# A convolution and spectral-mixing kernel: where the first transform's tiles run, a bank of transposes ahead of the last transform, and which engine clears two banks

## The chip, the cores and the metric

The kernel runs on one core of one Trainium2 chip. A time is the device time of one execution in microseconds (us). The core has five engines with queues of their own: TensorE (PE in the profile; its weight loads are PEld), VectorE (DVE), ScalarE (ACT), GpSimd (POOL) and SyncE (SP). [...] Matmul results land in PSUM, of which this kernel uses eight banks of 128 x 512 float32; VectorE and ScalarE read them out ("eviction").

## The reference

`x` is 8 x 3264 x 192 float32 (batch, row, channel). First a causal convolution with 7 taps runs along the rows; the 192 channels form 8 heads of 24, and the taps of a head are a softmax over 7 numbers. Then the first 64 frequencies of a real Fourier transform along the rows are mixed over channels with complex weights (64 matrices of 192 x 192, real and imaginary part), transformed back, added, and passed through a matrix with a rectifier:

```python
out = np.einsum('hk,bskhg->bshg', softmax(weight), x_unf)       # convolution, x = out
X = np.fft.rfft(x, axis=1)                                      # along the 3264 rows
Xr, Xi = np.real(X[:, :64]), np.imag(X[:, :64])
Yr = einsum('bmd,mde->bme', Xr, w_r) - einsum('bmd,mde->bme', Xi, w_i)
Yi = einsum('bmd,mde->bme', Xr, w_i) + einsum('bmd,mde->bme', Xi, w_r)
y = np.fft.irfft(Y, n=3264, axis=1)                             # Y is 0 above mode 63
u = x + y
result = u + np.maximum(u @ w_ch, 0.0)
```

## The kernel before

All work is bf16 in on-chip memory; the loads of `x` and of the weights are issued by GpSimd and change float32 into bf16 on the way. The order of the instructions on each engine is the order of the Python code (a manual schedule); semaphores only make an engine wait, they never reorder. The kernel has four stages.

*Convolution and forward transform.* The 8 batches are 4 pairs (`q` = 0 to 3), each cut into two units of row blocks; a block is 256 rows, and a pair has 26 tiles of 128 rows. Units 0 and 1 (pair 0) have 5 and 8 blocks, the others 7 and 6. GpSimd issues the loads of all units in order (`load_unit`, L152 and L156), then the weights. For each unit and head, `conv_step` makes eight short matmuls (L297) per half (`a` = 0, 1) against a band matrix, runs two steps behind itself for the upper rows (`CONVLAG = 2`), and evicts the result in place into `xall`: L334 on ScalarE or L336 on VectorE for pair 0, where one double-width PSUM tile holds both halves, L342 and L344 for the others, where each half has a bank of its own. Banks are taken from the front of the list `free` and put back at its end when evicted. For pair 0 the list holds four double banks, from unit 2 on eight single ones.

The forward transform of a pair is a sum over its 26 tiles of one matmul each (`dft`, L358) against the table `ftab` of sines and cosines. It is cut into two parts: the first goes to `xacc`, a stretch of `ct`, the second is added to it (L365). The table is made in six steps (`table`): steps 0 to 3 on VectorE (L197 to L204), the sine and cosine on ScalarE (L207, L209). `xtrans` (L377 to L388) turns the transformed rows and puts them into `xt`, the left operand of the mixing.

What stands around the change: 27 idle matmuls (L183) before the first convolution; after unit 0, ScalarE makes the first ten tiles' sines and cosines and TensorE runs 14 idle matmuls (L427). After unit 1, the PSUM pools are opened anew as eight single banks, in the order of their place and not of their release, and the ten tiles of unit 0 are transformed at once, into the first of these banks. The other 16 tiles of pair 0 follow after five heads of unit 2. For pairs 1 to 3 the parts are the tiles of their own two units; the last part of pair 3 (12 tiles) follows the last convolution.

*Transposes and mixing.* The pools are opened again: four banks for transposes (`zt4`), two (`ze`) and two (`zm`) for the mixing. Each mixing result fills only part of the partitions of `zm`, so two matmuls with a zero operand (L441) clear them. 16 groups of four modes (`mix`, L497, 24 matmuls for two groups) alternate with banks of transposes taken from a list (`tjobs`, L458): four banks of the table, one job that prepares `wsw`, and 39 banks of eight blocks of `xall`, written to `ct` (`c_bank`). A bank goes out by VectorE (L450) or, every third, by ScalarE (L448). Weights of groups 0 to 10 are loaded as early as there is room; group g + 11 is issued behind group g (L276). Each group's result passes through L507 or L509, a transpose, and L534 and L536 into `yet`.

*Way back.* Matmuls of `yet` with the channel matrix (L573, L574) begin after group 13 and run between groups 14 and 15.

*Output.* For each tile, L694 and L626 make the rectified and the plain part, L619 and L621 rectify, L606 adds, and SyncE stores.

Of the kernel before, what the change touches and what calls it, by code (L numbers as in the profile page):

```python
# [10 lines left out]
ACT = mybir.ActivationFunctionType  # L11
AX = mybir.AxisListType
F32 = mybir.dt.float32
BF16 = mybir.dt.bfloat16
# [6 lines left out]
def kernel(  # L21
# [9 lines left out]
    nc = tc.nc  # L31
    B, S, D = x.shape
    H, KK = weight.shape
# [4 lines left out]
    P = 128  # L38
    NQ = B // 2
    NB = S // (2 * P) + 1  # L40
    NT = 2 * NB
# [3 lines left out]
    BW = P + 2  # L45
    TWOPI = 6.283185
    MAGIC = 12582912.0
    NIDLE = 27
    UNITS0 = ((0, 5), (5, 8))
    UNITS = ((0, 7), (7, 6))  # L50
    units = [(q, b0, n) for q in range(NQ) for b0, n in (UNITS if q else UNITS0)]
# [11 lines left out]
    xall = sb("xall", [NSLOT, 2, D], BF16)  # L63
    ct = sb("ct", [NQ * NT * 3, P], BF16)
# [76 lines left out]

    ctx.enter_context(tc.manual_schedule())

    free = open_psum("left", (2, 2)) + open_psum("right", (2, 2))

    def load_unit(q, b0, n):
        nf = min(n, NB - 1 - b0)
# [44 lines left out]
    def table(step, t0, t1):  # L192

        n = t1 - t0
        tu, wh = tu3[:, t0:t1, :], wh3[:, t0:t1, :]
        if step == 0:
            nc.vector.tensor_tensor(out=tu, in0=sidx[:, t0:t1].unsqueeze(2).to_broadcast([P, n, MODES]),  # L197
                                    in1=midx.unsqueeze(1).to_broadcast([P, n, MODES]), op=ALU.mult)
        elif step == 1:
            nc.vector.tensor_scalar(out=wh, in0=tu, scalar1=MAGIC, scalar2=-MAGIC, op0=ALU.add, op1=ALU.add)  # L200
        elif step == 2:
            nc.vector.tensor_tensor(out=tu, in0=tu, in1=wh, op=ALU.subtract)
        elif step == 3:
            nc.vector.tensor_scalar(out=wh.bitcast(U32), in0=tu.bitcast(U32), scalar1=0x7FFFFFFF, scalar2=None,  # L204
                                    op0=ALU.bitwise_and)
        elif step == 4:
            nc.scalar.activation(out=ftab[:, t0:t1, 1:2 * MODES:2], in_=tu, func=ACT.Sin, scale=-TWOPI)  # L207
# [96 lines left out]
    def conv_step(u):  # L304

        lower = upper = iter(())
        flow.append(None)
        if u is not None:
            if u[0]:
                z = free.pop(0)  # L310
            else:
                z = flow[-2][0][2] if u[4] else free.pop(0)
            flow[-1] = [(u, z[:, u[4] if u[0] == 0 else 0, :], z), []]
            lower = conv_pieces(flow[-1][0], 0)
        old = flow[-1 - CONVLAG] if len(flow) > CONVLAG else None
# [12 lines left out]
        s0 = NT * q + 2 * b0  # L328
        dst = xall[:, s0:s0 + 2 * n, :, GRP * h:GRP * h + GRP].rearrange("p (b a) i e -> p a b i e", a=2)
        tile0 = flow[-2 - CONVLAG][0][2]  # L330
        if q == 0:
            srcv = tile0[:, :, 0:2 * GRP * n].rearrange("p a (b i e) -> p a b i e", b=n, i=2)
            if b0 == 0 or h % 2:
                nc.scalar.copy(out=dst, in_=srcv)  # L334
            else:
                nc.vector.tensor_copy(out=dst, in_=srcv)  # L336
            free.append(tile0)
        else:
            for a, z in enumerate((tile0, tile1)):
                srcv = z[:, 0, 0:2 * GRP * n].rearrange("p (b i e) -> p b i e", b=n, i=2)  # L340
                if a == 1:
                    nc.scalar.copy(out=dst[:, a], in_=srcv)  # L342
                else:
                    nc.vector.tensor_copy(out=dst[:, a], in_=srcv)  # L344
                free.append(z)

    def flush():
        for _ in range(CONVLAG):
            conv_step(None)
        flow.clear()  # L350

    def dft(q, t0, t1):

        z = free.pop(0)
        xp = z[:, 0, 0:2 * D]
        for t in range(t0, t1):
            k = PL if t >= NT - 2 else P
            nc.tensor.matmul(xp, ftab[0:k, t, :], xall[0:k, NT * q + t, :, :],  # L358
                             start=(t == t0), stop=(t == t1 - 1), skip_group_check=True)
        if t0 == 0 and q == 0:  # L360
            nc.vector.tensor_copy(out=xacc, in_=xp)
        elif t0 == 0:
            nc.scalar.copy(out=xacc, in_=xp)
        else:
            nc.vector.tensor_tensor(out=xs[q % 2][:, :, :].rearrange("p i d -> p (i d)"), in0=xp, in1=xacc, op=ALU.add)  # L365
        free.append(z)

    def xtrans(q, banks=None):
# [12 lines left out]
        for i in range(2):  # L381
# [5 lines left out]
            else:  # L387
                nc.scalar.copy(out=dst, in_=srcv)  # L388

    todo = []  # L390
    pend = []

    def dfts():
        while todo:
            q, t0, t1 = todo.pop(0)
            dft(q, t0, t1)
            if t1 == NT:
                pend.append(q)

    P1, P2 = (0, 2 * UNITS0[0][1]), (2 * UNITS0[0][1], NT)  # L400
    nc.vector.tensor_scalar(out=sidx, in0=sidx, scalar1=1.0 / S, scalar2=None, op0=ALU.mult)
    for part in (P1, P2):
        for step in range(4):
            table(step, *part)

    for k, u in enumerate(units):
        for h in range(H):
            for a in range(2):
                conv_step((*u, h, a))
            if k > 1 and h == (4 if k == 2 else 2):  # L410
                if pend:
                    xtrans(pend.pop(0))
                dfts()
        if k == 2:
            for g in range(NW + NL):
                load_w(g)
        todo.append((u[0], 2 * u[1], 2 * (u[1] + u[2])))
        if u[0]:
            continue

        flush()
        for step in (4, 5):
            table(step, *(P1, P2)[k])
        if k == 0:
            z = free.pop(0)
            for _ in range(14):
                nc.tensor.matmul(z[:, 0, :], band[:, 0, 0, 0:P], band[:, 0, 0:1, 0:P].to_broadcast([P, 4, P]), start=True,  # L427
                                 stop=True, skip_group_check=True)
# [4 lines left out]
    flush()  # L433
    dfts()
    nc.gpsimd.memset(yet[:, :, 2 * B * (MODES - 8):2 * B * MODES], 0.0)
    zt4 = open_psum("left", (1, 1, 1, 1))
# [1 line left out]
    ze, zm = [z[:, 0, :] for z in z4[0:2]], [z[:, 0, :] for z in z4[2:4]]  # L438
    for z in zm:

        nc.tensor.matmul(z[:, 0:2 * D], w1[0:64, 0:P], w1[0:64, :], start=True, stop=True, skip_group_check=True)  # L441
    tbank = [0]
    ncopy = [1]

    def copy(out, in_):
        ncopy[0] += 1
        if ncopy[0] % 3 == 0:
            nc.scalar.copy(out=out, in_=in_)  # L448
        else:
            nc.vector.tensor_copy(out=out, in_=in_)  # L450

    def next_bank():
        k = tbank[0] % 4
        tbank[0] += 1
        return zt4[k][:, 0, :].bitcast(BF16)

    def trans(o, in_):
        nc.tensor.matmul(o, in_, ident[:], start=True, stop=True, is_transpose=True)  # L458
# [7 lines left out]
    def c_bank(k0):  # L466
        tp = next_bank()
        for k in range(8):
            qt, w = divmod(k0 + k, 3)
            row = xall[:, qt, :, :].rearrange("p i d -> p (i d)")  # L470
            trans(tp[:, P * k:P * k + P], row[:, P * w:P * w + P])
        copy(ct[:, k0:k0 + 8, :].rearrange("p t s -> p (t s)"), tp[:, 0:8 * P])

    def w_bank():

# [307 lines left out]
```

## Time and profile before

| what | value |
|---|---|
| time, median of 3 runs (lowest to highest) | 174.47 us (174.03 to 174.59) |
| the profiled execution | 174.49 us, span 172.7 us |
| busy share of the span | PE 95%, DVE 74%, ACT 65%, POOL 32% |
| granted TensorE clock, mean | 0.996 |
| first convolution (L297) starts | 10.42 us |
| unit 1's convolution starts | 18.01 us |
| first mixing group (L497) starts | 74.81 us |
| HBM read, written | 39.10 MB, 20.05 MB |

The span runs from the first to the last instruction of the execution that was profiled; all positions in the text are microseconds from its start. A group line of the profile reads: line, engine, operation, output <- inputs, shapes, count, then busy time, mean duration in ns, and the idle time of that engine just before, with what ended it. A line of a timeline reads: start, duration, engine, line, operation, count, and in brackets the idle time before it and its releaser. Durations of matmuls overlap, so a group's extent over its count is the pace, not the mean. A line of the chain of waits is start, duration and what the path that ended last was doing there.

### The profile page before, as it was taken

The page shows a single profiled execution, that of the slowest core. Times are in us where ns is not written, and L with a number is a line of the kernel's source. Part 1 is how long each engine was busy: PE and PEld are TensorE (multiplying, and loading weights), DVE is VectorE, ACT ScalarE, POOL GpSimd, SP SyncE. Part 2 cuts the span into 40 slices and gives each one's busy share as a digit, 9 for nine tenths or more (in the row PEclk, how much of TensorE's full clock was granted, in tenths as well). Part 3 has the DMA queues.
Part 4 walks back from the last instruction along what each step waited for, and adds up shares of the span by engine and source line. Part 5 has one row for each costly group of instructions (what it writes and reads, how often), then busy time and mean ns, then how long its engine had stood idle before and what let it go on. Part 6 is the DMA issues. An engine that isn't in the chain of part 4 may idle for free.

```text
span 172.7 us, 6812 instructions
## 1 busy us (share of the span) xinstructions
PE 163.5 (95%) x2847; PEld 131.3 (76%) x2847; DVE 128.3 (74%) x258; ACT 112.6 (65%) x222; POOL 54.4 (32%) x93
## 2 busy tenths in 40 slices
PE   6999979999999999899999989999999999999980
PEld 2375757768778687589999965699899989999950
DVE  4899755457566584377777756799999999999990
ACT  8469177247366375177776744678888888878860
POOL 7999923324323354244441000890000000000000
PEclk9999999999999999999999999999999999999998
DMA  2999999999999999999999930489989899899995
GB/s 31 201 204 203 204 203 203 204 205 199 205 203 204 208 207 209 203 207 206 206 207 207 206 58 0 156 289 342 339 314 360 313 349 353 321 351 332 352 344 188
DMA packets 37359, 40.14 MB, mean 232 GB/s; under 512 B 2480, under 2 KB 37328, under 8 KB 37328
## 3 DMA queue, kind: packets, MB, share of 16 engines
q0 software_dynamic: 22816, 19.62, 70.9%
q1 hardware_dynamic: 14512, 20.09, 31.8%
q8 instruction: 22, 0.36, 0.8%
q14 instruction: 9, 0.07, 0.1%
HBM read 39.10 MB, written 20.05 MB: 342 GB/s over the span
## 4 chain that ended last, share of the span: by engine, by line
PE 82%; DMA 7%; DVE 3%; POOL 2%; ACT 2%; issue 1%; DVEq 0%; POOLq 0%; ACTq 0%
PE z L694 34%; PE z L297 18%; PE z L458 11%; PE z L358 10%; DMA xall<-in_x_dram 7%; PE z L497 3%; POOL xall L152 2%; DVE xall L344 1%; PE z L626 1%; PE z L573 1%; PE z L574 1%; PE z L377 1%; DVE arena L606 1%; PE z L564 1%; ACT ftab L448 1%
## 5 line engine op out<-in xcount | busy, mean ns | idle before, releaser
L606 DVE TENSOR_TENSOR arena<-z,xall 128x384 f32<-128x384 f32 (+1 forms) x104 | 57.0, 557 | 3.8 <-PE z L694 1.9
L619 ACT ACTIVATE z<-z 128x384 f32<-128x384 f32 x102 | 48.2, 475 | 12.8 <-PE z L694 3.7
L694 PE MATMUL z<-arena,ftab 64*128 64x384 bf16 x308 | 45.3, 322 | 0.0
L694 PEld LDWEIGHTS <-ct 64*128 64x128 bf16 x600 | 42.3, 94 | 3.3 <-PE z L626 0.6
L297 PE MATMUL z<-xall,shared 64*64 64x336 bf16 (+3 forms) x1024 | 37.9, 294 | 0.2 <-DMA xall<-in_x_dram 0.2
L694 PE MATMUL z<-wsw,ct 64*128 64x192 bf16 x300 | 37.4, 243 | 0.0
L297 PEld LDWEIGHTS <-shared 64*64 64x64 bf16 x1024 | 32.7, 106 | 5.7 <-issue 2.9
L694 PE MATMUL z<-wm,ct 64*128 64x192 bf16 x200 | 31.4, 243 | 0.0
L344 DVE CAST xall<-z 128x336 bf16<-128x336 f32 (+1 forms) x48 | 22.9, 483 | 11.1 <-PE z L297 8.8
L694 PEld LDWEIGHTS <-ftab 64*128 64x128 bf16 x396 | 28.7, 93 | 2.8 <-issue 1.0
L342 ACT CAST xall<-z 128x336 bf16<-128x336 f32 (+1 forms) x48 | 20.1, 419 | 13.2 <-PE z L297 8.4
L694 PE MATMUL z<-w,ct 64*128 64x192 bf16 x100 | 24.3, 243 | 0.0
L450 DVE COPY ct<-z 128x1024 bf16<-128x1024 bf16 x26 | 17.8, 689 | 5.7 <-PE z L458 4.2
L458 PE MATMUL z<-ident,xall 128*128 128x128 bf16 x312 | 19.9, 219 | 0.0
L358 PE MATMUL z<-xall,ftab 128*128 128x384 bf16 (+1 forms) x104 | 18.3, 326 | 1.4 <-ACT xall L334 0.9
L458 PEld LDWEIGHTS <-xall 128*128 128x128 bf16 x312 | 17.8, 98 | 0.9
L152 POOL DMA_DIRECT2D xall<-in_x_dram x16 | 14.9, 939 | 6.9 <-DMA xall<-in_x_dram 6.0
L448 ACT COPY ct<-z 128x1024 bf16<-128x1024 bf16 x13 | 13.2, 1013 | 4.9 <-PE z L458 4.9
L358 PEld LDWEIGHTS <-ftab 128*128 128x128 bf16 (+1 forms) x104 | 9.7, 98 | 8.7 <-issue 2.7
L694 PE MATMUL z<-mixa,ftab 64*128 64x384 bf16 x88 | 13.8, 323 | 0.1
L521 POOL DMA_DIRECT2D arena<-xs x16 | 7.9, 504 | 17.1 <-ACT xs L517 17.1
L334 ACT CAST xall<-z 128x480 bf16<-128x480 f32 (+1 forms) x12 | 7.0, 660 | 5.9 <-PE z L297 5.9
(112 smaller groups left out, 153.9 us busy)
## 6 DMA issues: line engine op xcount, KB each, us to landing
out_dram<-arena SPq DMA_DIRECT2D x47, 384.0 KB, 3.5
xall<-in_x_dram POOLq DMA_DIRECT2D x8, 672.0 KB, 16.1
xall<-in_x_dram POOLq DMA_DIRECT2D x8, 480.0 KB, 16.7
arena<-in_moe_w_r_dram POOLq DMA_DIRECT2D x10, 288.0 KB, 11.3
arena<-in_moe_w_i_dram POOLq DMA_DIRECT2D x10, 288.0 KB, 11.3
ct<-in_moe_w_r_dram POOLq DMA_DIRECT2D x6, 288.0 KB, 11.7
ct<-in_moe_w_i_dram POOLq DMA_DIRECT2D x6, 288.0 KB, 11.9
out_dram<-arena SPq DMA_DIRECT2D x3, 288.0 KB, 2.9
```

What stands on the lines that cost most here:

```text
L152: nc.gpsimd.dma_start(out=xin[:, s0:s0 + nf, 2 * D * i:2 * D * (i + 1)], in_=src)
L297: yield nc.tensor.matmul(o, band[r, h, int(a != a1), c0:c0 + 64], xin5[r, s1:s1 + n, :, a1, dsl], start=(row == 0 and a1 == 0), stop=(row ...
L342: nc.scalar.copy(out=dst[:, a], in_=srcv)
L344: nc.vector.tensor_copy(out=dst[:, a], in_=srcv)
L358: nc.tensor.matmul(xp, ftab[0:k, t, :], xall[0:k, NT * q + t, :, :], start=(t == t0), stop=(t == t1 - 1), skip_group_check=True)
L448: nc.scalar.copy(out=out, in_=in_)
L450: nc.vector.tensor_copy(out=out, in_=in_)
L458: nc.tensor.matmul(o, in_, ident[:], start=True, stop=True, is_transpose=True)
L521: nc.gpsimd.dma_start(out=zwl[k:k + 1, :, :, :].rearrange("p b t d -> p b (t d)"), in_=ylate[r + 2:r + B, :])
L606: nc.vector.tensor_tensor(out=o[0:pn, :, a, :], in0=bank[0:pn, 0:2 * D].rearrange("p (i d) -> p i d", i=2), in1=xall[0:pn, s + a, :, :], o ...
L619: nc.scalar.activation(out=z, in_=z, func=ACT.Relu)
L694: mm = nc.tensor.matmul(target(bank[k], cols, r), l, r, start=first, stop=last, skip_group_check=True)
```

## The change

Five edits, named by the lines before:

- The forward transform of pair 0 is cut at tile 6 instead of tile 10. Its first part (`PA`, six tiles) runs directly after unit 0, between four and three idle matmuls in place of 14; `xacc` is then written by ScalarE. The other 20 tiles run at the place in unit 2 where 16 ran. Nothing is transformed between units 1 and 2.
- The table is made in three parts (6, 10 and 10 tiles) whose steps are spread: VectorE makes `PA` before the first eviction, the others between and behind the evictions of unit 0; ScalarE makes the sine of `PA` after its fifth eviction.
- In unit 0 heads 5 and 7 are evicted by VectorE instead of ScalarE; in unit 1 the even heads go to ScalarE and the odd ones to VectorE, the other way round than before. The opening has 24 idle matmuls instead of 27.
- After unit 1 the eight single banks are listed in the order in which their double banks came free.
- One `c_bank` (blocks 8 to 15) runs between the last convolution and the last transform, in a bank of the list `free`, and leaves the list `tjobs`. The two clearing matmuls become two ScalarE activations of scale 0. `copy` counts this bank, so that in the mixing stage the copies change engine one bank later than before.

```diff
-    NIDLE = 27
+    NIDLE = 24
-    free = open_psum("left", (2, 2)) + open_psum("right", (2, 2))
+    twos = open_psum("left", (2, 2)) + open_psum("right", (2, 2))
+    free = list(twos)
...
-            if b0 == 0 or h % 2:
+            if h not in (5, 7) if b0 == 0 else h % 2 == 0:
                 nc.scalar.copy(out=dst, in_=srcv)
...
-        if t0 == 0 and q == 0:
-            nc.vector.tensor_copy(out=xacc, in_=xp)
-        elif t0 == 0:
+        if t0 == 0:
             nc.scalar.copy(out=xacc, in_=xp)
...
+    def c_bank(k0, tp=None):
+        tp = next_bank() if tp is None else tp
...
-    P1, P2 = (0, 2 * UNITS0[0][1]), (2 * UNITS0[0][1], NT)
+    PA, PB, PC = (0, 6), (6, 16), (16, NT)
     nc.vector.tensor_scalar(out=sidx, in0=sidx, scalar1=1.0 / S, scalar2=None, op0=ALU.mult)
-    for part in (P1, P2):
-        for step in range(4):
-            table(step, *part)
+    for step in range(4):
+        table(step, *PA)
+    chores = {(0, 0): [(PB, (0,))], (0, 5): [(PA, (4,))], (0, H): [(PA, (5,)), (PB, (1, 2, 3)), (PC, range(4))],
+              (1, H): [(PC, (4, 5))]}
+    def tables(*place):
+        for part, steps in chores.get(place, ()):
+            for step in steps:
+                table(step, *part)
...
             for a in range(2):
                 conv_step((*u, h, a))
+            tables(k, h)
...
         flush()
-        for step in (4, 5):
-            table(step, *(P1, P2)[k])
+        tables(k, H)
         if k == 0:
-            z = free.pop(0)
-            for _ in range(14):
-                nc.tensor.matmul(z[:, 0, :], band[:, 0, 0, 0:P], ...
-            free.append(z)
+            idle(4)
+            dft(0, *PA)
+            for step in (4, 5):
+                table(step, *PB)
+            idle(3)
         else:
-            free[:] = open_psum("left", (1, 1, 1, 1)) + open_psum("right", (1, 1, 1, 1))
-            dft(*todo.pop(0))
+            ones = open_psum("left", (1, 1, 1, 1)) + open_psum("right", (1, 1, 1, 1))
+            free[:] = [ones[2 * twos.index(z) + i] for z in free for i in range(2)]
+            todo.append((0, PA[1], NT))
     flush()
+    z = free.pop(0)
+    c_bank(8, z[:, 0, :].bitcast(BF16))
+    free.append(z)
     dfts()
...
     for z in zm:
-        nc.tensor.matmul(z[:, 0:2 * D], w1[0:64, 0:P], w1[0:64, :], start=True, stop=True, skip_group_check=True)
+        nc.scalar.activation(out=z[:, 0:2 * D], in_=ident[:, 0:1].to_broadcast([P, 2 * D]), func=ACT.Copy, scale=0.0)
...
-    tjobs += [(c_bank, k) for k in range(0, 3 * NT * NQ, 8)]
+    tjobs += [(c_bank, k) for k in range(0, 3 * NT * NQ, 8) if k != 8]
```

`idle(n)` is the loop of idle matmuls as a function of their number.

More of the change, by code (lines that the diff above doesn't have):

```diff
@@ L388, in xtrans, with copy, trans @@
                 nc.scalar.copy(out=dst, in_=srcv)
+    ncopy = [1]
+    def copy(out, in_):
+        ncopy[0] += 1
+        if ncopy[0] % 3 == 0:
+            nc.scalar.copy(out=out, in_=in_)
+        else:
+            nc.vector.tensor_copy(out=out, in_=in_)
+    def trans(o, in_):
+        nc.tensor.matmul(o, in_, ident[:], start=True, stop=True, is_transpose=True)
+    def c_bank(k0, tp=None):
+        tp = next_bank() if tp is None else tp
+        for k in range(8):
+            qt, w = divmod(k0 + k, 3)
+            row = xall[:, qt, :, :].rearrange("p i d -> p (i d)")
+            trans(tp[:, P * k:P * k + P], row[:, P * w:P * w + P])
+        copy(ct[:, k0:k0 + 8, :].rearrange("p t s -> p (t s)"), tp[:, 0:8 * P])
     todo = []
@@ L398, in dfts, with idle @@
                 pend.append(q)
-    P1, P2 = (0, 2 * UNITS0[0][1]), (2 * UNITS0[0][1], NT)
+    PA, PB, PC = (0, 6), (6, 16), (16, NT)
     nc.vector.tensor_scalar(out=sidx, in0=sidx, scalar1=1.0 / S, scalar2=None, op0=ALU.mult)
-    for part in (P1, P2):
-        for step in range(4):
-            table(step, *part)
+    for step in range(4):
[6 more added lines that the diff above has]
+                table(step, *part)
+    def idle(n):
+        z = free.pop(0)
+        for _ in range(n):
+            nc.tensor.matmul(z[:, 0, :], band[:, 0, 0, 0:P], band[:, 0, 0:1, 0:P].to_broadcast([P, 4, P]), start=True,
+                             stop=True, skip_group_check=True)
+        free.append(z)
     for k, u in enumerate(units):
@@ L416 @@
                 load_w(g)
-        todo.append((u[0], 2 * u[1], 2 * (u[1] + u[2])))
         if u[0]:
+            todo.append((u[0], 2 * u[1], 2 * (u[1] + u[2])))
             continue
         flush()
-        for step in (4, 5):
-            table(step, *(P1, P2)[k])
+        tables(k, H)
         if k == 0:
-            z = free.pop(0)
-            for _ in range(14):
-                nc.tensor.matmul(z[:, 0, :], band[:, 0, 0, 0:P], band[:, 0, 0:1, 0:P].to_broadcast([P, 4, P]), start=True,
-                                 stop=True, skip_group_check=True)
-            free.append(z)
-        else:
-            free[:] = open_psum("left", (1, 1, 1, 1)) + open_psum("right", (1, 1, 1, 1))
-            dft(*todo.pop(0))
+            idle(4)
[3 more added lines that the diff above has]
+            idle(3)
+        else:
+            ones = open_psum("left", (1, 1, 1, 1)) + open_psum("right", (1, 1, 1, 1))
+            free[:] = [ones[2 * twos.index(z) + i] for z in free for i in range(2)]
+            todo.append((0, PA[1], NT))
     flush()
+    z = free.pop(0)
+    c_bank(8, z[:, 0, :].bitcast(BF16))
+    free.append(z)
     dfts()
@@ L439 @@
     for z in zm:
-        nc.tensor.matmul(z[:, 0:2 * D], w1[0:64, 0:P], w1[0:64, :], start=True, stop=True, skip_group_check=True)
+        nc.scalar.activation(out=z[:, 0:2 * D], in_=ident[:, 0:1].to_broadcast([P, 2 * D]), func=ACT.Copy, scale=0.0)
     tbank = [0]
[L443 to L450, printed above, removed]
     def next_bank():
@@ L455, in next_bank @@
         return zt4[k][:, 0, :].bitcast(BF16)
-    def trans(o, in_):
-        nc.tensor.matmul(o, in_, ident[:], start=True, stop=True, is_transpose=True)
     def g_bank(t0, n):
@@ L464, in g_bank @@
         copy(ftab[:, t0:t0 + n, :].rearrange("p t s -> p (t s)"), tp[:, 0:P * n])
[L466 to L472, printed above, removed]
     def w_bank():
```

## The prediction

> **What bounds the kernel now.** I read the page first (busy time, slices, chain by line), then the chain of waits piece by piece, then the timelines of single engines around each edit, last the issues and landings of the weight loads.
>
> ```profile
> PE 163.5 (95%) x2847; PEld 131.3 (76%) x2847; DVE 128.3 (74%) x258; ACT 112.6 (65%) x222; POOL 54.4 (32%) x93
> ...
> GB/s 31 201 204 203 204 203 203 204 205 199 205 203 204 208 207 209 203 207 206 206 207 207 206 58 0 156 289 342 339 314 360 313 349 353 321 351 332 352 344 188
> ...
> PE z L694 34%; PE z L297 18%; PE z L458 11%; PE z L358 10%; DMA xall<-in_x_dram 7%; PE z L497 3%; POOL xall L152 2%; DVE xall L344 1%; PE z L626 1%; PE z L573 1%; PE z L574 1%; PE z L377 1%; DVE arena L606 1%; PE z L564 1%; ACT ftab L448 1%
> ```
>
> TensorE is busy 95% and its lines carry the chain; work taken off it before the output stage looks worth its full length. But the GB/s row is flat at about 205 from slice 2 to slice 23 (some 99 us): the loads of x and then of the weights run without a hole, whatever TensorE does. So the question is how close the weights' landings lie to the matmuls that use them (L497). Its last groups in TensorE's timeline, with what ScalarE does between them:
>
> ```profile
> 96.58 0.70 PE L497 MATMUL z<-arena,mixa 128*16 128x192 bf16 x24
> ...
> 98.32 1.01 ACT L448 COPY ct<-z 128x1024 bf16<-128x1024 bf16 x1 [0.48 <-PE z L458]
> ...
> 99.23 0.27 ACT L536 COPY yet<-z 128x128 bf16<-128x128 bf16 x1
> ...
> 100.28 0.47 PE L497 MATMUL z<-arena,mixa 128*16 128x192 bf16 x12
> ...
> 103.61 0.46 PE L497 MATMUL z<-arena,mixa 128*16 128x192 bf16 x12
> ```
>
> The first row is groups 12 and 13 of the 16 weight groups (12 matmuls each), so group 13 starts 0.35 in, at 96.93; the others are groups 14 and 15. The second half of group 13 was issued at 84.98, that of group 15 at 91.05 (GpSimd's timeline), and the issue view gives their times to landing:
>
> ```profile
> 84.98 0.61 POOL L276 DMA_DIRECT2D arena<-in_moe_w_i_dram  x1 [0.56 <-DMA ct<-in_moe_w_i_dram]
> ```
> ```profile
> 91.05 0.61 POOL L276 DMA_DIRECT2D arena<-in_moe_w_i_dram  x1 [0.55 <-DMA arena<-in_moe_w_i_dram]
> ```
> ```profile
> arena<-in_moe_w_i_dram POOLq DMA_DIRECT2D x1, 288.0 KB, 11.5
> ```
> ```profile
> arena<-in_moe_w_i_dram POOLq DMA_DIRECT2D x1, 288.0 KB, 11.1
> ```
>
> Group 13 is complete at 84.98 + 11.5 = 96.5, group 15 at 91.05 + 11.1 = 102.2, group 14 about halfway, at 99.3. The slack before the matmuls is 0.4, 1.0 and 1.4 us. That is the core of this prediction: TensorE can come early by 0.4 us at group 13 and not more.
>
> **The change, part by part.** GpSimd's and SyncE's queues keep their instructions, their order and their waits; each weight issue waits for the landing eight loads earlier (the releasers above), so nothing here makes the loads end sooner.
>
> *Six tiles in the wait for rows.*
>
> ```profile
> 24.16 0.81 ACT xall L334
> ...
> 25.02 1.78 PE z L358 x10
> 26.80 2.97 PE z L297 x72
> ```
> ```profile
> 14.58 3.19 PE L427 MATMUL z<-shared 128*128 128x512 bf16 x14
> 18.01 6.12 PE L297 MATMUL z<-xall,shared 64*64 64x384 bf16 x128 [0.23 <-DMA xall<-in_x_dram]
> ```
> ```profile
> 11.60 3.80 ACT L334 CAST xall<-z 128x480 bf16<-128x480 f32 x8 [1.38 <-PE z L297]
> 15.43 0.92 ACT L207 ACTIVATE ftab<-arena 128x640 bf16<-128x640 f32 x1
> ```
>
> Between 14.58 and 18.01 TensorE runs 14 idle matmuls (0.23 each) until rows land. After: 4 idle ones (to 15.5), six tiles (1.78/10 = 0.178 each, 1.1), 3 idle ones. The tiles need cosines: five evictions (0.475 each, to 14.0), a sine for six tiles (between 0.92 x 384/640 = 0.55 and 0.92; 0.63 taken), the seventh eviction, a cosine: ready at about 15.75, tiles done at 16.9, idle ones at 17.6. The rows' landing hides all this; only 0.4 us of slack is left, and what runs over 18.0 delays the second unit one for one. Three of the opening 27 idle matmuls go; the first convolution waits for ScalarE's bands, so at most 0.1, swallowed by the same landing.
>
> *The second unit and what follows.*
>
> ```profile
> L152 POOL DMA_DIRECT2D xall<-in_x_dram x2: 957/974/992, 6.3 to 7.2; - x2
> ...
> DMA to landing us min/median/max: 14.6/15.8/17.0
> ```
>
> Now the convolution ends at 24.13, the eviction at 24.16 holds its bank until 25.0, ten tiles run, and unit 2 starts at 26.8. After the change nothing stands between: banks are taken in the order in which they came free, and unit 2 starts when its rows are in, at 7.2 + 17.0 = 24.2, say 24.35. Gain 2.4. Four of these ten tiles move into the second pair's transform (20 tiles for 16): 4 x 0.178 = 0.7 back. ScalarE now makes the last ten tiles' sines and cosines (two of about 0.95) as unit 2 starts, and its first eviction there comes late by up to 1 us; eight banks absorb between all and half of that: 0 to 0.5. Front gain 1.2 to 1.7; I take 1.5. Evictions that alternate engines the other way, and the DVE table steps spread behind them, I cost at nothing: the convolution between 18.0 and 24.1 covers them, with a ring of four double banks; were the ring full, each microsecond of a late eviction would be one on the path.
>
> *The last transform.*
>
> ```profile
> 69.79 2.11 PE L358 MATMUL z<-xall,ftab 128*128 128x384 bf16 x12 [0.55 <-DVE xall L344]
> 71.83 0.49 PE L441 MATMUL z<-w 64*128 64x384 bf16 x2
> ```
> ```profile
> 72.01 0.56 DVE L365 TENSOR_TENSOR xs<-z,ct 128x384 bf16<-128x384 f32 x1 [2.27 <-PE z L358]
> ```
> ```profile
> 73.36 1.01 ACT L448 COPY ftab<-z 128x1024 bf16<-128x1024 bf16 x1 [3.69 <-PE z L458]
> 74.27 0.48 ACT L388 CAST mixa<-z 128x384 bf16<-128x384 f32 x1
> ```
> ```profile
> 106.85 0.47 ACT L619 ACTIVATE z<-z 128x384 f32<-128x384 f32 x1 [0.85 <-PE z L626]
> ```
>
> ```profile
> L450 DVE COPY ct<-z 128x1024 bf16<-128x1024 bf16 x26 | 17.8, 689 | 5.7 <-PE z L458 4.2
> L458 PE MATMUL z<-ident,xall 128*128 128x128 bf16 x312 | 19.9, 219 | 0.0
> ```
>
> Eight transposes now fill the 0.55 us in which TensorE waits for the last evictions (eight take 8 x 19.9/312 = 0.5): no cost, and one bank less later. The two clearing matmuls (0.43 on the path) go to ScalarE, but one cleared bank is the one the last transform used, so the clears wait for DVE's sum, 72.01 + 0.56 = 72.57. Two clears of that shape (0.47 each by the nearest row, 0.4 at least) end at 73.4, when the table copy starts today (73.36); then comes the 0.48 copy that releases the first L497. So this edit gains 0 (from -0.2 to +0.1).
>
> *The mixing stage.* TensorE enters it 1.5 us early, runs as tightly as before (copies alternate in another phase, same load), reaches group 13 at 95.4 and waits for its landing: start 96.5, not 96.93, which is 0.4 kept and 1.1 lost. From there to group 14 one bank of transposes fewer remains. Today ScalarE's 1.01 copy at 98.32 delays its L536 copy to 99.23, which the next matmuls wait for. After, ScalarE copies the first of two banks and DVE the second, in 0.69. Counted from the end of group 13, DVE's part is ready at 1.0 + 0.7 + 0.2 = 1.9 against ScalarE's 2.2 today (99.50 - 97.28), so about 0.25 more is gained. Group 14 then starts at about 99.65, after its landing (99.3); group 15 follows 3.3 later at 102.95, after 102.2. The rest is the same work.
>
> **Sum:** 0.4 + 0.2 = 0.6 us off the profiled 174.49 (span 172.7 and 1.8 around it; the median of the runs is 174.47): 173.9. With landings 0.3 earlier or later, 173.5 to 174.2. About 0.3%, 0.52 us, is what a measurement of this kernel can tell from no change, so this sits at that edge.
>
> [...]
>
> **Rivals.**
> *A, no floor:* the loads move with TensorE or the landings I read are not what L497 waits for. Then 1.5 plus one bank (0.5) stays: 174.49 - 2.0 = 172.5. Against it: eight loads in flight and a flat rate. Chance 0.17.
> *B, a later floor:*
>
> ```profile
> q8 instruction: 22, 0.36, 0.8%
> ```
>
> Code fetches take 0.8% of 16 x 172.7 us over 22 packets, 1.0 us of one engine each. One more ahead of a last piece puts a landing up to 1 us later; before, slack hid that, now nothing does: up to 174.8, no measurable change. Chance 0.18.
> *C, slower: a slow clock.* The opening idle matmuls show two rates (the first six, then the last seven):
>
> ```profile
> L183 PE MATMUL z<-xall 128*128 128x512 bf16 x6 | 2.7, 630 | 1.6 <-DVE xall L170 1.6
> ```
> ```profile
> L183 PE MATMUL z<-xall 128*128 128x512 bf16 x7 | 1.7, 379 | 0.0
> ```
>
> 0.45 against 0.24 us each. Fewer idle matmuls, and three waits of up to 0.7 us (one for the three taken off the opening, two about the six tiles), could drop TensorE to the slow rate. Unit 1 (6.1 us) would then take up to 5.2 more: 174.49 - 1.5 + 5.2 - 0.25 = 177.9. It decides for slower once over 2.3 us are lost, about 2.7 us at the slow rate. Against: after the opening no gap of the trace shows it. Chance 0.13 (with other losses of that size).
> [...]
>
> **How the numbers follow.** The forecast has 0.52, of which 0.35 lies below 173.95 (0.3% faster) and 0.17 within. Faster: 0.35 + A 0.17 = 0.52. Same: 0.17 + B 0.18 = 0.35. Slower: C, 0.13. The range runs from A's 172.5, taken at 172.6, to B's 174.9.
>
> **What would show it.** Right: unit 2's convolution starts at 24.3 to 24.5; the first L497 at about 73.3; TensorE waits about 1 us for a weight load between groups 12 and 13, at 96.5; the weight issues and landings stay within 0.3 us. Wrong: group 13 runs at 95.4 without a wait (A); landings later (B); unit 1's matmuls above 6.3 us (C); or clears on ScalarE that end long after 73.4 - 1.5, which the 1.1 us wait would still hide.

## The result, and the profile after

The kernel after takes 173.91 us (median of 11 executions, 173.75 to 174.48) against 174.55 us (174.03 to 175.01, 11 executions) before: ratio 0.9968, 95% interval 0.9954 to 0.9982, so 0.64 us or 0.3% faster. The profiled execution took 174.37 us (span 172.6 us) and is one of the longer ones; its positions are used here, not its total.

On the profile page of the kernel after, the busy times, the data rate in 40 slices, and the chain by engine and by line:

```profile
PE 160.3 (93%) x2835; PEld 129.5 (75%) x2835; DVE 128.4 (74%) x263; ACT 113.0 (65%) x225; POOL 51.8 (30%) x93
...
GB/s 29 201 204 203 204 204 205 202 203 202 204 202 207 206 206 206 207 206 209 203 206 208 205 63 0 177 308 337 345 338 348 343 330 346 340 323 304 384 327 156
...
PE 53%; DMA 35%; DVE 3%; POOL 3%; issue 3%; ACT 0%; DVEq 0%; POOLq 0%
PE z L713 34%; DMA ct<-in_moe_w_i_dram 14%; PE z L298 10%; DMA arena<-in_moe_w_r_dram 7%; DMA xall<-in_x_dram 7%; DMA arena<-in_moe_w_i_dram 6%; PE z L359 5%; POOL xall L153 2%; PE z L592 1%; PE z L645 1%; DVE xall L345 1%; PE z L593 1%; PE z L516 1%; PE z L583 1%; DVE arena L625 1%
```

The chain by engine on the page of the kernel before:

```profile
PE 82%; DMA 7%; DVE 3%; POOL 2%; ACT 2%; issue 1%; DVEq 0%; POOLq 0%; ACTq 0%
```

TensorE is 3.2 us less busy (163.5 to 160.3), and the kernel is 0.6 us shorter. The rate row is as flat as before, up to the same slice. What changed is the chain: before, its 7% of DMA were loads of `x` and no load of a weight was among its listed lines; now weight loads hold 27% of the span (14 + 7 + 6). That is the share of the path traced back through one load to the one before it, not idle time of TensorE. The stretch around group 13 in the chain of waits of the kernel after (start, duration, what):

```profile
85.24 11.18 DMA arena<-in_moe_w_i_dram
96.42 0.04 issue
96.47 0.49 PE z L516 x11
```

The load lands at 96.42, and the matmuls start 0.05 us later. TensorE's timeline after, from the first transform to the last mixing group (L298 is the convolution, L359 the transform, L516 the mixing):

```profile
15.23 1.14 PE L359 MATMUL z<-xall,ftab 128*128 128x384 bf16 x6 [0.30 <-DVE xall L337]
...
17.97 4.80 PE L298 MATMUL z<-xall,shared 64*64 64x384 bf16 x104 [0.96 <-DMA xall<-in_x_dram]
23.00 4.48 PE L298 MATMUL z<-xall,shared 64*64 64x384 bf16 x96 [0.22 <-DVE xall L337]
27.41 3.42 PE L359 MATMUL z<-xall,ftab 128*128 128x384 bf16 x20
30.77 3.46 PE L298 MATMUL z<-xall,shared 64*64 64x336 bf16 x96
...
68.15 2.12 PE L359 MATMUL z<-xall,ftab 128*128 128x384 bf16 x12
...
73.31 0.71 PE L516 MATMUL z<-arena,mixa 128*16 128x192 bf16 x24 [1.00 <-ACT mixa L387]
...
94.90 0.46 PE L516 MATMUL z<-arena,mixa 128*16 128x192 bf16 x12
96.47 0.46 PE L516 MATMUL z<-arena,mixa 128*16 128x192 bf16 x12 [1.11 <-DMA arena<-in_moe_w_i_dram]
99.78 0.46 PE L516 MATMUL z<-arena,mixa 128*16 128x192 bf16 x12
103.09 0.46 PE L516 MATMUL z<-arena,mixa 128*16 128x192 bf16 x12
```

Between the units there is no transform any more (23.00 to 27.41 is the end of unit 1 and the start of unit 2 without a hole). The mixing starts 1.50 us earlier (73.31, before 74.81). TensorE came 1.50 us earlier, yet the second half of group 13 was issued 0.26 us later (85.24, before 84.98) and was complete at the same time (96.42, before 96.48). So 1.11 us of idle TensorE stand ahead of group 13, and group 15 starts only 0.52 us earlier (103.09, before 103.61). Most of the gain was handed back at this one wait.

### The profile page after: what moved, and what is told of

Same layout as the page of the kernel before. It is cut to its first block, busy times and chain, and to the rows that moved or that the text cites. A ratio compares the mean times of both kernels' runs of the same rounds, so it can differ in the third digit from the quotient of the medians.

```text
span 172.6 us, 6803 instructions
## 1 busy us (share of the span) xinstructions
PE 160.3 (93%) x2835; PEld 129.5 (75%) x2835; DVE 128.4 (74%) x263; ACT 113.0 (65%) x225; POOL 51.8 (30%) x93
## 4 chain that ended last, share of the span: by engine, by line
PE 53%; DMA 35%; DVE 3%; POOL 3%; issue 3%; ACT 0%; DVEq 0%; POOLq 0%
PE z L713 34%; DMA ct<-in_moe_w_i_dram 14%; PE z L298 10%; DMA arena<-in_moe_w_r_dram 7%; DMA xall<-in_x_dram 7%; DMA arena<-in_moe_w_i_dram 6%; PE z L359 5%; POOL xall L153 2%; PE z L592 1%; PE z L645 1%; DVE xall L345 1%; PE z L593 1%; PE z L516 1%; PE z L583 1%; DVE arena L625 1%
## 5 line engine op out<-in xcount | busy, mean ns | idle before, releaser
L298 PE MATMUL z<-xall,shared 64*64 64x336 bf16 (+3 forms) x1024 | 38.3, 294 | 1.6 <-DMA xall<-in_x_dram 1.0
L298 PEld LDWEIGHTS <-shared 64*64 64x64 bf16 x1024 | 33.0, 106 | 7.3 <-issue 4.1
L713 PE MATMUL z<-wsw,ct 64*128 64x192 bf16 x300 | 35.1, 243 | 0.0
L713 PEld LDWEIGHTS <-ftab 64*128 64x128 bf16 x396 | 29.7, 93 | 2.7 <-issue 0.5
L713 PE MATMUL z<-wm,ct 64*128 64x192 bf16 x200 | 29.9, 243 | 0.0
L713 PE MATMUL z<-w,ct 64*128 64x192 bf16 x100 | 24.3, 243 | 0.0
L359 PE MATMUL z<-xall,ftab 128*128 128x384 bf16 (+1 forms) x104 | 18.3, 327 | 0.3 <-DVE xall L337 0.3
L359 PEld LDWEIGHTS <-ftab 128*128 128x128 bf16 (+1 forms) x104 | 9.6, 98 | 7.6 <-issue 0.8
L394 ACT COPY ct<-z 128x1024 bf16<-128x1024 bf16 x12 | 12.1, 1012 | 1.3 <-PE z L399 1.1
L277 POOL DMA_DIRECT2D arena<-in_moe_w_r_dram x10 | 6.1, 614 | 10.7 <-PE z L399 4.3
```

The lines of the kernel that those rows point to most:

```text
L298: yield nc.tensor.matmul(o, band[r, h, int(a != a1), c0:c0 + 64], xin5[r, s1:s1 + n, :, a1, dsl], start=(row == 0 and a1 == 0), stop=(row ...
L713: mm = nc.tensor.matmul(target(bank[k], cols, r), l, r, start=first, stop=last, skip_group_check=True)
```

## The experiments

The theory is the prediction's: weights land on a clock of their own, and TensorE may come to group 13 earlier by 0.4 us and no more. Rival A says that there is no such floor, rival B that it moves, rival C that idle TensorE lowers the granted clock. Some expectations name one more, the store theory: the stores of the output stage swallow small shifts ahead of them, so that the time stays while group 15 moves. Each ratio below is against the kernel before, run on the same chip in the same job. A row stands for 12 executions, except after (11), before_few_loads (9), before_delay4 and banks_in_wait (5 each) and after_few_loads (4).

| kernel | median us | ratio | 95% interval |
|---|---|---|---|
| after | 173.91 | 0.9968 | 0.9954 to 0.9982 |
| delay4 | 173.91 | 0.9974 | 0.9959 to 0.9989 |
| delay9 | 174.34 | 0.9994 | 0.9977 to 1.001 |
| before_delay4 | 175.54 | 1.0057 | 1.0044 to 1.007 |
| banks_in_wait | 173.67 | 0.9947 | 0.9933 to 0.996 |
| banks_in_wait_2 | 173.44 | 0.995 | 0.993 to 0.997 |
| after_few_loads | 172.64 | 0.9893 | 0.9878 to 0.9908 |
| before_few_loads | 173.97 | 0.9977 | 0.9962 to 0.9991 |
| front_only | 174.76 | 1.0008 | 0.9993 to 1.0023 |
| front_few_loads | 173.91 | 0.9973 | 0.9956 to 0.9989 |
| tail_only | 174.36 | 0.9985 | 0.997 to 0.9999 |
| tail_few_loads | 173.99 | 0.997 | 0.995 to 0.999 |
| no_idle | 174.54 | 1.0003 | 0.9982 to 1.0023 |

### Work added ahead of the floor

If a wait of 1.1 us is really slack, TensorE can be given that much useless work in front of it for nothing, while the kernel before pays for it in full. The runs delay4 and delay9 are the kernel after with four and nine such matmuls, before_delay4 is the kernel before with four. The edit, near the start of the mixing, with 4 or 9 matmuls of 512 columns:

```diff
         mix_trans(d, 0, 2)
         some(3)
+        if d == 0:
+            z = zt4[tbank[0] % 4][:, 0, :]
+            for _ in range(4):
+                nc.tensor.matmul(z, ident[:], ident[:].unsqueeze(1).to_broadcast([P, 4, P]), start=True, stop=True, ...
```

> Four idle matmuls (0.22 us each, 0.9 together) are put on TensorE in the changed kernel, early in the mixing stage behind group 1. Floor theory (the landing of the weights of group 13 sets the end, TensorE waits 1.1 us there): they vanish in that wait, group 13 still starts at 96.5, group 15 at 103.1, time 173.9 as for the changed kernel. Path theory (what TensorE does ahead counts in full): 174.8. Store theory (the stores of the output stage swallow small shifts): time 173.9 too, but group 15 at 104.0.

> Nine idle matmuls (1.95 us) at the same place. Floor theory: 1.1 of them vanish, group 13 starts at 97.3, group 15 at 103.9, time 174.75. Path theory: 175.85. Store theory: group 15 at 105.0, time below 174.5.

> Four idle matmuls (0.9 us) at the same place of the kernel before, whose group 13 starts 0.4 us after its weights. Floor theory: no wait to vanish in, so the full 0.9: 175.4. Path theory: the same 175.4. Store theory: 174.5.

TensorE's timelines at groups 12 and 13, first of the kernel after with four:

```profile
96.08 0.46 PE L516 MATMUL z<-arena,mixa 128*16 128x192 bf16 x12
97.02 0.46 PE L516 MATMUL z<-arena,mixa 128*16 128x192 bf16 x12 [0.48 <-DMA arena<-in_moe_w_i_dram]
```

then of the kernel after with nine:

```profile
96.76 0.71 PE L516 MATMUL z<-arena,mixa 128*16 128x192 bf16 x24
```

and of the kernel before with four:

```profile
97.38 0.70 PE L497 MATMUL z<-arena,mixa 128*16 128x192 bf16 x24
```

From the first mixing matmul to group 12 the kernel after took 21.59 us (94.90 - 73.31); with four it took 0.90 more and with nine 1.95 more; the kernel before with four took 0.87 more. In the time, four cost the kernel before 0.57%, 1.0 us, and the kernel after 0.06%, which is inside the intervals. Nine use the wait up (the row is one of 24 matmuls, without a wait) and cost 0.26%, about 0.45 us, half of the 1.95 - 1.11 = 0.84 that the wait of the profiled execution leaves uncovered; the intervals allow both. Rival A is refuted: without a floor, nine would have cost 1.95. The store theory fails too: by it, before_delay4 would have stayed at 174.5, and it took 175.54; and with nine, group 15 starts at 103.63, not at 105.0.

The row with four shows something else: the weights of group 13 land at 96.97 there (the matmuls start at 97.02), 0.55 us later than in the kernel after. Such a movement is what rival B forecast, and it is met again below.

### The late loads left out

> The changed kernel without the loads of weight groups 11 to 15: these groups use the weights of groups 0 to 4, which still lie in their places, so modes 44 to 63 are mixed with other weights. Nothing else is left out. Floor theory: the wait at group 13 is gone, it starts at 95.2 and group 15 at 101.7, time about 172.5, some 1.4 below the changed kernel. Store theory (the output stage's stores swallow what is gained ahead of it): group 15 at 101.7 but time not below 173.5.

> The kernel before without the loads of groups 11 to 15, with the same part of the computation changed. Floor theory: it never waited for these loads, so 174.4 to 174.5, unchanged; against it the full change is then worth 1.9 us. Store theory: unchanged too, but the change is worth at most 1 us against it.

```diff
-            for half, src in ((0, moe_w_r), (1, moe_w_i)):
+            for half, src in ((0, moe_w_r), (1, moe_w_i)) if g < NW + NL else ():
```

TensorE's timeline of the kernel after without the loads of groups 11 to 15:

```profile
94.89 0.70 PE L516 MATMUL z<-arena,mixa 128*16 128x192 bf16 x24
98.44 0.46 PE L516 MATMUL z<-arena,mixa 128*16 128x192 bf16 x12
101.76 0.46 PE L516 MATMUL z<-arena,mixa 128*16 128x192 bf16 x12
```

and of the kernel before without them:

```profile
96.29 0.71 PE L497 MATMUL z<-arena,mixa 128*16 128x192 bf16 x24
...
103.32 0.46 PE L497 MATMUL z<-arena,mixa 128*16 128x192 bf16 x12
```

Groups 12 and 13 run back to back, and the kernel after takes 172.64 us, close to the 172.5 of the forecast without a floor; the store theory had it at 173.5 or more. The change is worth 173.97 - 172.64 = 1.33 us where nothing bounds it, and 0.64 where the landing does. The expectation was 1.9, and it was missed on the side of the kernel before: that one was to stay at 174.4 to 174.5 and also gained 0.23%, 0.4 us, though it had no wait to lose: unit 1 starts 0.30 us earlier in that profiled execution. Whether the missing loads are the cause of that was not separated.

### The parts alone, with and without the floor

"Front" is the change without the bank of transposes ahead of the last transform (all 39 banks are in the list) and with the two clearing matmuls left on TensorE; "tail" is the kernel before with just these edits.

```diff
 (front: the kernel after, less)
-    z = free.pop(0)
-    c_bank(8, z[:, 0, :].bitcast(BF16))
-    free.append(z)
...
-        nc.scalar.activation(out=z[:, 0:2 * D], in_=ident[:, 0:1].to_broadcast([P, 2 * D]), func=ACT.Copy, scale=0.0)
+        nc.tensor.matmul(z[:, 0:2 * D], w1[0:64, 0:P], w1[0:64, :], start=True, stop=True, skip_group_check=True)
```

> The changed kernel with the last three edits undone: no bank of transposes ahead of the last transform, the two clearing matmuls back on TensorE, all 39 banks in the list. Floor theory: the last transform starts at 68.15 as in the changed kernel, group 13 waits until 96.5, group 14 and 15 keep the old distance, group 15 at 103.15, time 174.0. Path theory (the front counts in full): 172.9.

> The kernel before with only the last three edits: one bank of transposes ahead of the last transform, ScalarE clears the two banks, the bank leaves the list. Floor theory: the first group starts 0.1 later (74.9), group 13 at 97.05 after its weights, group 15 at 103.5, time 174.35. Path theory (0.43 of clearing and 0.5 of transposes leave TensorE): 173.55.

> The change's front alone (no bank of transposes ahead of the last transform, TensorE clears the banks) without the loads of weight groups 11 to 15; the output is wrong, since these groups are mixed with the weights of earlier ones. Theory: the front's gain is real and front_only lost it at the landing of group 13's weights. Against the kernel before without the same loads (0.9977 of before) this kernel is then 0.9 to 1.1 us shorter: 173.0 to 173.2, ratio 0.991 to 0.993, mixing from about 73.7. Rival: the front gives nothing to the end of the kernel, with or without the floor: 173.9 to 174.1.

> The change's tail alone (the bank of transposes ahead of the last transform, ScalarE clears the banks) without the loads of groups 11 to 15; output wrong as above. Theory: the tail saves 0.3 ahead of the mixing and 0.3 behind group 13: 173.4, ratio 0.994. Rival (the prediction's own sizes, nothing ahead of the mixing): 0.25 to 0.3 below the kernel before without the loads, 173.7, ratio 0.996.

TensorE's timeline of front_only:

```profile
68.42 2.11 PE L359 MATMUL z<-xall,ftab 128*128 128x384 bf16 x12 [0.55 <-DVE xall L345]
...
73.78 0.71 PE L513 MATMUL z<-arena,mixa 128*16 128x192 bf16 x24 [0.35 <-ACT mixa L387]
...
96.94 0.46 PE L513 MATMUL z<-arena,mixa 128*16 128x192 bf16 x12 [0.91 <-DMA arena<-in_moe_w_i_dram]
...
103.71 0.46 PE L513 MATMUL z<-arena,mixa 128*16 128x192 bf16 x12
```

and of tail_only:

```profile
69.33 2.13 PE L358 MATMUL z<-xall,ftab 128*128 128x384 bf16 x12
...
74.07 0.71 PE L501 MATMUL z<-arena,mixa 128*16 128x192 bf16 x24 [0.15 <-issue]
...
96.58 0.46 PE L501 MATMUL z<-arena,mixa 128*16 128x192 bf16 x12 [0.44 <-DMA arena<-in_moe_w_i_dram]
```

The tail's time came as expected (174.35, measured 174.36), but not by the expected way: the mixing was to start at 74.9 and group 13 at 97.05 without a wait, and they start at 74.07 and 96.58 behind a wait of 0.44. So that agreement is luck. The front's time did not come as expected: 174.0 was expected and nothing measurable gained. The rows hold three reasons. First, the front enters the mixing 1.03 us early, not 1.5: from the last transform's start to the mixing it takes 5.36 us (73.78 - 68.42) where the kernel before takes 5.02. Second, its weights landed late in this execution, at 96.89. Third, a group 13 that waits and so runs alone takes 0.46 us instead of the 0.35 it adds behind group 12. With the landing at 96.45, group 15 would start at 103.71 - 0.44 = 103.27, a gain of 0.34 us; the interval (-0.07% to +0.23%) still excludes that.

Without the late loads the parts show up in the trace, but not in the time. Positions in us, from TensorE's timelines:

| without late loads | unit 1 starts | mixing starts | group 15 starts | unit 1 to group 15 | span |
|---|---|---|---|---|---|
| before | 17.71 | 74.52 | 103.32 | 85.61 | 172.20 |
| front | 18.18 | 73.86 | 102.67 | 84.49 | 172.58 |
| tail | 17.73 | 74.27 | 102.75 | 85.02 | 171.79 |
| after | 17.93 | 73.28 | 101.76 | 83.83 | 170.85 |

From unit 1's start to group 15 the front takes 1.12 us off, the tail 0.59 and both 1.78: they add up. The ratios do not: against 0.9977, the front's 0.9973 is 0.1 us and the tail's 0.997 another 0.1, both together 1.3 (by the medians) to 1.5. By the intervals, each of these differences is known to about 0.4 us. The expectations of 173.1 and 173.4 were missed by 0.8 and 0.6. Part of it lies behind group 15: from its start to the end of the span these four took 68.88, 69.91, 69.04 and 69.09 us. In the front's execution, 64.27 of that run to TensorE's last matmul (before 63.77) and 5.64 from there to the end (before 5.11). But these are single executions; front and tail ran in another job than the other two, and what takes their gain back was not found. It stays open, and with it how much of the 0.64 us each part of the change contributes.

### Filling the wait

In the kernel after TensorE waits 1.1 us for group 13 and then transposes three banks that depend on no weight, two directly behind it and one a little later. Putting these banks between the groups:

```diff
     mix(2 * d, zm[0])
+    some(99)
     mix(2 * d + 1, zm[0])
     mix_copy(d, zm[0], 0, 2)
-    some(2)
     mix_trans(d, 0, 2)
-    some(99)
```

> The changed kernel with its last three banks of transposes put between groups 12 and 13, into the wait. Floor theory: 1.1 us of this work is free there; group 13 starts at 96.8, group 14 right after its weights at 99.3, group 15 at 102.6, time 0.5 lower: 173.4. Path theory: the same work in another order, 173.9. Store theory: group 15 at 102.6 but time 173.9.

> The same kernel as banks_in_wait a second time: the banks of transposes behind group 13's copy run in the wait ahead of it. If the 0.2 to 0.4 below the changed kernel was real, the ratio to before is 0.994 to 0.996 again; if it was the jitter of the rows' and the weights' landings, 0.996 to 0.998 like the changed kernel.

TensorE's timeline of banks_in_wait_2:

```profile
94.97 0.46 PE L516 MATMUL z<-arena,mixa 128*16 128x192 bf16 x12
96.81 0.46 PE L516 MATMUL z<-arena,mixa 128*16 128x192 bf16 x12
99.35 0.46 PE L516 MATMUL z<-arena,mixa 128*16 128x192 bf16 x12
102.66 0.47 PE L516 MATMUL z<-arena,mixa 128*16 128x192 bf16 x12
```

Group 13 starts 0.34 us later than in the kernel after and without a wait, and group 14 already 2.54 us behind it instead of 3.31, which leaves group 15 0.43 earlier. In the profiled execution of the first run (banks_in_wait) group 15 starts at 103.19, no earlier than in the kernel after; there unit 2 had waited 0.67 us for its rows, and the mixing started 0.58 us later (73.89). On two chips the ratio is 0.9947 and 0.995, 0.75 to 0.9 us below the kernel before: the fastest kernel of the study that leaves no load out. Against the kernel after it was not run side by side, and the intervals overlap, so that the further gain is likely but not shown.

### Without the idle matmuls in the wait for rows

```diff
         if k == 0:
-            idle(4)
             dft(0, *PA)
             for step in (4, 5):
                 table(step, *PB)
-            idle(3)
```

> The changed kernel without the seven idle matmuls in the wait for the rows. Theory: they cover nothing that the end waits for, and the clock stays: ratio to before 0.995 to 0.998, mean clock as in the changed kernel, group 13's matmuls at its weights' landing. Rival (the rival of the slow clock): with 0.8 to 1.7 us more of an idle TensorE the granted clock falls for a stretch behind the wait, unit 1's convolution takes over 6.5 instead of 6.1 us a group of 128, and the time is 175 or more.

TensorE's timeline of no_idle:

```profile
15.62 1.14 PE L359 MATMUL z<-xall,ftab 128*128 128x384 bf16 x6 [1.65 <-DVE xall L337]
...
68.63 2.12 PE L359 MATMUL z<-xall,ftab 128*128 128x384 bf16 x12
...
72.94 0.71 PE L514 MATMUL z<-arena,mixa 128*16 128x192 bf16 x24 [0.16 <-issue]
...
96.82 0.47 PE L514 MATMUL z<-arena,mixa 128*16 128x192 bf16 x12 [1.81 <-DMA arena<-in_moe_w_i_dram]
...
99.35 0.37 PE L590 MATMUL z<-wm,yet 128*128 128x192 bf16 x1
...
104.39 0.47 PE L514 MATMUL z<-arena,mixa 128*16 128x192 bf16 x12
```

Busy time by stretches of the same execution (stretch, length, busy time and count of PE, PEld, DVE, ACT and POOL, and as the last three values the granted TensorE clock, where 1.00 is full speed, DMA share and GB/s):

```profile
7.00:18.00 11.00, 7.57 (x144) 5.02 (x142) 10.59 (x30) 7.30 (x17) 9.51 (x22) 1.00 1.31 204
18.00:25.00 7.00, 6.39 (x130) 5.15 (x132) 5.42 (x8) 4.23 (x7) 2.52 (x3) 1.00 1.31 204
...
96.00:104.00 8.00, 6.79 (x87) 5.47 (x88) 2.36 (x6) 3.17 (x7) 0.00 (x0) 0.79 0.69 117
```
```profile
99.00:100.00 1.00, 1.00 (x11) 0.98 (x9) 0.60 (x3) 0.05 (x1) 0.00 (x0) 0.50 1.00 169
```

and the same stretch of the kernel after:

```profile
96.00:104.00 8.00, 6.67 (x109) 5.11 (x110) 3.29 (x7) 3.98 (x9) 0.00 (x0) 1.00 0.68 117
```

Both expectations failed in the time; only group 13's start at its weights' landing came as the first had it. The place where rival C was looked for, in and behind the wait for rows, keeps its full clock (1.00 in 7 to 18 and in 18 to 25). But the list of banks now turns by two places fewer, the clears of the last transform find a bank that is free, and the mixing starts at 72.94. So TensorE waits 1.81 us at group 13 instead of 1.11, and behind that wait the clock is halved: 0.50 at 99 to 100, 0.79 over the eight microseconds, which at 0.50 is 8 x 0.21 / 0.5 = 3.4 us (by single microseconds 0.58, 0.50, 0.50 and 0.71 from 98 to 102, and 1.00 in the two before and the two behind). A matmul of the way back takes 0.37 us instead of 0.25, and group 13 to group 15 takes 7.57 us instead of 6.62. Group 15 starts 1.30 us later than in the kernel after: 0.95 for that, and 0.35 because the weights of group 13 landed later in this execution. Of the twelve executions, two had a mean granted clock of 0.995 or more and took 173.52 and 173.54 us; the eight between 0.973 and 0.983 took 174.04 to 175.14, and the two between these (0.988 and 0.989) 175.10 and 174.69. In the kernel after all eleven lie between 0.988 and 0.997, like the kernel before (0.989 to 0.999), so its 1.11 us wait did not set this off.

What exactly set it off stays open. In the same execution TensorE waited 1.65 us ahead of the six tiles (the first row) and 1.40 us ahead of unit 1, with 1.14 us of work between them, and kept its full clock (1.00 in both stretches). Whether the length of a single wait decides was not shown: there are two values, 1.65 us with the full clock behind it and 1.81 with half of it, from one profile.

## Why the prediction was right

**The time.** 0.6 us was forecast and 0.64 measured, with an interval of 0.31 to 0.80; in the profiled execution, 0.52 stood at group 15. Of the forecast's two terms, the 0.4 at group 13 came (0.46: 96.93 to 96.47), and the 0.2 behind it hardly did (0.06). That the medians differ by 0.64 and not by 0.5 was not traced, so it is luck that the total agrees this closely.

**The floor (the core of it): right.** Group 13's weights land at 96.42 (forecast 96.5), the matmuls follow at 96.47, the wait is 1.11 us (forecast "about 1 us"). Useless work of 0.9 us in front of it costs nothing that could be measured; without the late loads the gain doubles. Rival A is refuted. The issues of the last ten half-group loads moved by -0.28 to +0.48 us, somewhat more than the 0.3 of the forecast, and not with TensorE's 1.50.

**Six tiles in the wait for rows: right in its cost, off in its detail.** Tiles run from 15.23 to 16.4 (forecast 15.75 to 16.9) and unit 1 starts with its rows, at 17.97 (before 18.01). One cost that I set to nothing is a wait: in unit 1 TensorE stands 0.22 us at 23.00 for a VectorE eviction. VectorE's table steps end at 19.63 there and it stood idle before this eviction, so the table is not what held it up; why TensorE meets this wait is not shown. In banks_in_wait this wait is 0.76 (at 21.55). In the kernel after it was hidden by the rows of unit 2: they land at 24.30, and unit 2 starts at 24.41 (forecast 24.3 to 24.5).

**The second unit: right.** Two rows of the kernel before show the same places as 27.41 and 30.77 above:

```profile
29.70 2.77 PE L358 MATMUL z<-xall,ftab 128*128 128x384 bf16 x16
32.41 3.46 PE L297 MATMUL z<-xall,shared 64*64 64x336 bf16 x96
```

The tiles of unit 2 begin 2.29 us earlier (forecast 2.4), the four more cost 3.36 - 2.71 = 0.65 (forecast 0.7), so the front gains 1.64 (forecast 1.2 to 1.7, 1.5 taken).

**The last transform: right in size, and the reason it is worth more elsewhere was missed.** From its start to the mixing the kernel after takes 5.16 us (73.31 - 68.15) and the kernel before 5.02: a loss of 0.14, inside the -0.2 to +0.1 given. ScalarE's timelines show why, first after, then no_idle:

```profile
71.03 0.90 ACT L480 ACTIVATE z<-ident 128x384 f32<-128x384 bf16 x2 [3.00 <-DVE xs L364]
```
```profile
68.69 0.90 ACT L478 ACTIVATE z<-ident 128x384 f32<-128x384 bf16 x2 [0.18 <-DVE xall L345]
```

As forecast the clears wait for VectorE's sum, since the first of them has the transform's bank. With another turn of the list they run 2.3 us earlier, and the same edits take 4.74 us (tail_only) or 4.31 us (no_idle). The order of the banks is worth up to 0.85 us in this stage (5.16 - 4.31), more than the 0.43 us that the two clearing matmuls took on TensorE's path.

**The mixing stage behind group 13: the term was mis-sized.** 0.25 us was forecast between groups 13 and 14. The step was 3.35 us before (96.93 to 100.28) and is 3.31 after, 0.04 less. Where group 13 does not wait it is 98.44 - 95.24 = 3.20 (the kernel after without late loads; group 13 is 0.35 into its row). The shorter copy gives 0.15, and a group 13 that runs alone takes 0.46 instead of 0.35 and gives 0.11 of it back; that I had not counted.

**Rival B: the landing does move, and its cause is not shown.** In the profiled executions in which TensorE waited for it, the second half of group 13 was complete between 96.42 (after) and 96.97 us (delay4). Group 15 moves with it (103.09 and 103.65); the forecast's bounds of 0.3 on each side of 96.5 were exceeded twice, by 0.1 (front_only) and 0.2 us (delay4). That code fetches are the cause was only argued: the pages of the kernels before and after have the same 22 packets in their row of the instruction queue (q8).

**Rival C did not come true for this change:** the clock of the kernel after is 1.00 in every stretch from 7 to 168 us. A slow clock came in a neighbouring kernel and in another place: not where idle matmuls were taken away, but behind the wait at group 13, when that wait grew to 1.81 us. Nor is the opening's slow rate, from which this rival took its size, shown to be one of the granted clock: that is 1.00 in 1.6 to 4.3 us of the kernel before, where six idle matmuls took 0.45 us each, and in 9 to 10.4, where the last ones took 0.24.

## What to carry to other kernels

When a chain on TensorE is shortened, look for the next thing with a clock of its own, here a stream of loads at a flat rate, and read its landings against the instructions that wait for them: the smallest slack, 0.4 us, bounded a gain of 1.6. Independent work that stands behind such a wait belongs in front of it (by the ratios about another 0.3 us here, with overlapping intervals), and arriving there still earlier can cost: in one kernel the clock was halved behind a wait of 1.81 us there. Which buffer a list hands out next can be worth as much as the edit that changed the order, so follow the buffers through every stage behind a change.

## What the runs showed that was not expected

- The granted clock fell to 0.50 behind a wait of 1.81 us, about 1.3 us after its end (0.83 in 98 to 98.25, 0.50 from 98.25 to 101.5, 0.85 in 101.5 to 101.75, then 1.00), and stayed there for about 3.4 us; behind waits of 1.11 us (kernel after) and 1.65 us (the same execution) it stayed at 1.00.
- The output stage is not a constant. From group 15's start to the end of the span the profiled executions took from 68.55 (delay4) to 69.91 us (tail_only, front_few_loads). In the kernel after, TensorE's last row is the first below, in the kernel before the second; it ends 0.92 us earlier, and the span is only 0.1 shorter:

```profile
166.12 0.75 PE L645 MATMUL z<-arena,ftab 128*128 128x384 bf16 x2
```
```profile
167.10 0.69 PE L626 MATMUL z<-arena,ftab 128*128 128x384 bf16 x2
```

  What lies between is the last stores. For those that SyncE issues from 164 us on, the issue view gives the median from issue to landing, for the last two after and then before:

```profile
out_dram<-arena SPq DMA_DIRECT2D x2, 144.0 KB, 3.8
```
```profile
out_dram<-arena SPq DMA_DIRECT2D x2, 144.0 KB, 3.0
```

  So 0.8 of the 0.92 us were lost there, for a reason that the profile does not show. From TensorE's last matmul to the end of the span the executions took 4.74 to 6.00 us. This spread of over 1 us is larger than the change, so a single span says little here, and only medians of several executions are compared.
